# Moving the key and value loads of batches 1 to 7 from the ScalarE queue to the SyncE queue in a fused attention and mixture-of-experts kernel

## The chip, the cores and the metric

The kernel runs on one core of one Trainium2 chip. The metric is the device time of one execution in microseconds (us), as the median over runs. One further execution was taken by the hardware profiler; every time below that is not called a run's time comes from that profile and counts from the start of its span.

## What is computed

Two stages, the second fed by the first:

```
q: (8, 16, 384, 64)   k, v: (8, 1, 384, 64)      # 16 query heads share one key/value head
attn = softmax(q @ k^T / 8) @ v                  # per batch and head
x    = attn laid out as (8*384, 16*64) = (3072, 1024)

g    = argmax(x @ w_group)                       # 4 groups, top 1
e    = argmax(x @ w_expert[g])                   # 4 experts in the group, top 1
out  = p_group * p_expert * (relu(x @ w1[g,e]) @ w2[g,e])     # w1, w2: 1024 x 1024 each
```

All inputs and the output are fp32. For each token only the chosen expert counts.

## The kernel before

The work is tiled by batch (8 batches of 384 tokens) and, within a batch, by three query chunks of 1024 columns. The program walks over 24 chunks; its loop variable is `p` (L409), with `b, r = divmod(p, 3)` the batch and the chunk within it, and `g = 2 * p` and `g + 1` the two halves of the chunk. The order of instructions on each engine is written out by hand (the pools are under a manual schedule), so a queue runs its instructions in the order in which the program text issues them.

One pass through the loop does, in this order:

- `scores` (L188) for half `g`, key tiles 0 and 1: TensorE multiplies keys by queries into the PSUM tile `s` (two buffers), and ScalarE takes the exponential into `pt` (L195). A third `s` tile has to wait until ScalarE has read the first.
- `stats_q` (L161): one ScalarE pass over the raw queries of `p`. After it, `load_q(p + 3)` (L73) issues four DMAs from SyncE into the raw-query buffer that `p` used (three buffers, so the load waits for `stats_q(p)` and for the transpose of `p`).
- Where r is 1: `gate_a` (L271), the router's matmuls for the batch before, with a ScalarE copy.
- On VectorE: `pre_add` (L200, adds the exponentials of the key tiles into `presum`), `prep_q(p + 1)` (L179, transposes the next chunk's queries into `qT`) and, where r is 2, `prep_k(b + 1)` (L175, the next batch's keys into `kT`).
- On TensorE: `values` (L249, `pt` times `v`) for the previous chunk, and the softmax denominators of the previous chunk. Up to chunk 6 these come from `sum_keys` (L223: matmuls into `kss`, transposed by VectorE into `krow`, L230) and `invert` (L233: small matmuls `sm` from `krow`, L238, then a reciprocal and a transpose). From chunk 7 on, VectorE folds the sums instead (`fold_keys`, L213).
- `scores` for key tile 2 of half `g` and tile 0 of half `g + 1`, then `weigh(p - 1)` (L258), which writes the attention output `xT`, a bf16 copy of it by GpSimd and, at the end of a batch, a store of it to DRAM from SyncE (L267).
- From chunk 7 on (`MOE_AT`, L408), `fill` (L398) puts units of the expert stage between the attention pieces: `h_unit` (L348, eight matmuls with `w1` and a ReLU on ScalarE) and `y_unit` (L357, eight matmuls with `w2`, a scaled copy on ScalarE, and a store of `y` from SyncE, L380).
- `scores` for key tiles 1 and 2 of half `g + 1`. Where r is 1, `gate_c` (L319) finds the expert that most tokens of the batch before chose and has GpSimd load that expert's weights (L95, L331).
- At the end of the pass, where r is 0: `load_kv(b + 1)` (L83). It issues four key DMAs (48 KB each, the keys written twice into a layout of 32-row pieces) and one value DMA (96 KB). Keys and values have two buffers each. The keys are transposed two passes later by `prep_k(b + 1)`, and the values are first read four passes later, by `values`.

Batch 0's keys are loaded from ScalarE before the loop and its values from SyncE. All other loads of keys and values go from ScalarE, behind the exponentials of the pass and ahead of those of the next. Queries, the router's weights (`gw`, L152 to L154), the stores of `x_bf` and all stores of `y` go from SyncE; expert weights go from GpSimd.

The framework gives the DMAs of SyncE and ScalarE together eight completion semaphores, by turns, in the order in which it plans them. A DMA that gets a semaphore waits on its own engine until the DMA that had the semaphore before has landed. The listing of the kernel's instructions shows these waits; for batch 3, loaded at the end of pass 6, the four key DMAs and the value DMA wait in ScalarE's stream for the semaphores numbered 6, 0, 1, 2 and 3, and numbers 2 and 3 were last given to the first two of the four query loads of chunk 9, which SyncE issues in the same pass.

Of the kernel before, what the change touches and what calls it, by code (L numbers as in the profile page):

```python
# [21 lines left out]
def kernel(  # L22
# [11 lines left out]
    nc = tc.nc  # L34
# [7 lines left out]
    ST = S // P  # L42
# [16 lines left out]
    kv = k.rearrange("b o (k i) (j d) -> b o j i k d", i=32, j=2)  # L59
# [23 lines left out]
    def load_kv(b):  # L83
        kt = pool.tile([P, NB, 32], FP32, tag="k", name="k")
        for a in range(2):
            for j in range(2):
                nc.scalar.dma_start(out=kt[64 * a + 32 * j:64 * a + 32 * j + 32], in_=kv[b, 0, j])
        k_raw[b] = kt
        vt = pool.tile([P, ST, D], FP32, tag="v", name="v")
        (nc.sync if b == 0 else nc.scalar).dma_start(out=vt[:], in_=v[b, 0].rearrange("(st p) d -> p st d", st=ST))  # L90
        v_sb[b] = vt

    def load_w1(w1, e):
# [10 lines left out]
    make_identity(nc, ident)  # L104
    load_q(0, 2)
    load_kv(0)

    one = singles.tile([P, 1], FP32, name="one")
# [300 lines left out]
    for p in range(NP + 1):  # L409
        b, r = divmod(p, RP)  # L410
# [80 lines left out]
        if r == 0 and b + 1 < B:  # L491
            load_kv(b + 1)
# [262 lines left out]
```

## Time and profile before

The runs take 509.71 us in the median (508.79 to 510.08, three runs). The profiled execution has a span of 507.9 us.

| engine | busy, us | share of the span |
|---|---|---|
| TensorE matmul (PE) | 482.7 | 95% |
| TensorE weight load (PEld, overlaps PE) | 205.1 | 40% |
| VectorE (DVE) | 345.0 | 68% |
| ScalarE (ACT) | 241.6 | 48% |
| GpSimd (POOL) | 63.7 | 13% |

In the lines of the profile, a group or a piece of the timeline is named by engine, source line, operation and `out<-in` tiles, `xN` being how many instructions are merged. In the timeline the first number is the start and the second the duration, both in us; in brackets stands how long the engine sat idle before and what ended it. `ACTq` and `SPq` are the issuing of DMAs on those engines, which the busy time does not count. In the table of waits the three numbers are the total in us, how many waits, and the longest. `PEclk` is the granted TensorE clock as a share of full speed.

### The profile page before, as it was taken

The numbers are of one execution on the slowest core, as the hardware profiler recorded it, in microseconds if no ns is written. First come the engines' busy times: TensorE is split into PE (matmuls) and PEld (weight loads), VectorE is DVE, ScalarE is ACT, GpSimd is POOL, SyncE is SP. The second block draws the span as 40 slices with busy tenths as digits, with TensorE's granted clock in tenths as the row PEclk, the third lists the DMA queues.
The fourth block names the chain that finished last, engine by engine and source line by source line (L and its number), as shares of the span: only waits on it lengthen the run. The fifth ranks groups of instructions, "written<-read, shape, count | busy, mean of one in ns | idle before, by whom it ended". The sixth has DMA issues, their size and how long they took to land. (4 is left out here: it accounts for less than half of the span.)

```text
span 507.9 us, 6898 instructions
## 1 busy us (share of the span) xinstructions
PE 482.7 (95%) x2603; PEld 205.1 (40%) x2623; DVE 345.0 (68%) x480; ACT 241.6 (48%) x341; POOL 63.7 (13%) x64
## 2 busy tenths in 40 slices
PE   8899999969999999999999999999999999998893
PEld 5233333324433443344433444344443444455451
DVE  4588789649974897859975997779974984332100
ACT  4555555245445555545644555454744642322241
POOL 1011113101110020101110120101110210210000
PEclk9999999979999999999999999999999999999997
DMA  9492619963995389845993399647951296599990
GB/s 127 50 126 43 128 29 175 208 129 43 210 183 187 44 139 216 204 87 89 214 205 118 63 182 199 188 83 125 218 129 63 61 205 128 166 245 246 228 243 25
DMA packets 148440, 73.04 MB, mean 144 GB/s; under 512 B 122651, under 2 KB 122651, under 8 KB 148400
## 3 DMA queue, kind: packets, MB, share of 16 engines
q0 software_dynamic: 19008, 37.84, 41.3%
q1 hardware_dynamic: 113792, 32.43, 31.0%
q10 hardware_dynamic: 15600, 2.26, 2.6%
q8 instruction: 22, 0.36, 0.3%
q14 instruction: 18, 0.15, 0.1%
HBM read 91.31 MB, written 19.40 MB: 218 GB/s over the span
## 5 line engine op out<-in xcount | busy, mean ns | idle before, releaser
L195 ACT ACTIVATE pt<-s 128x1024 f32<-128x1024 f32 x144 | 139.8, 1022 | 136.0 <-PE s L193 113.7
L193 PE MATMUL s<-qT,kT 64*128 64x512 f32 x576 | 145.4, 624 | 4.3 <-ACT pt L195 3.4
L256 PE MATMUL o<-pt,v 128*64 128x512 f32 x576 | 130.4, 598 | 0.0
L203 DVE TENSOR_TENSOR presum<-pt 128x1024 f32<-128x1024 f32 x48 | 63.6, 1325 | 46.9 <-ACT pt L195 46.9
L353 PE MATMUL hps<-xbf,w 128*128 128x384 bf16 x512 | 89.3, 326 | 3.8 <-DVE rarei L633 2.0
L362 PE MATMUL yps<-w,hT 128*128 128x512 bf16 x365 | 86.8, 379 | 2.6 <-ACT y L364 1.3
L265 POOL CAST xbf<-xT 128x1024 bf16<-128x1024 f32 x24 | 40.7, 1696 | 326.9 <-DVE xT L264 326.9
L193 PEld LDWEIGHTS s<-qT,kT 64*128 64x128 f32 x576 | 49.3, 187 | 65.0 <-issue 40.6
L256 PEld LDWEIGHTS o<-pt,v 128*64 128x64 f32 x576 | 38.6, 136 | 87.2 <-issue 80.3
L353 PEld LDWEIGHTS <-w 128*128 128x128 bf16 x512 | 48.8, 99 | 46.0 <-issue 16.2
L207 DVE TENSOR_TENSOR presum<-presum,pt 128x1024 f32<-128x1024 f32 x48 | 58.5, 1220 | 2.5
L364 ACT ACTIVATE y<-yps,gsel 128x512 f32<-128x512 f32 x48 | 32.9, 686 | 54.8 <-PE yps L362 48.4
L362 PEld LDWEIGHTS <-hT 128*128 128x128 bf16 x384 | 37.1, 100 | 52.3 <-issue 14.5
L355 ACT ACTIVATE hT<-hps 128x384 bf16<-128x384 f32 x64 | 31.4, 491 | 43.5 <-PE hps L353 41.1
L215 DVE STREAM_TRANSPOSE turn<-presum 128x1024 f32<-128x1024 f32 x34 | 42.3, 1245 | 1.2
L219 DVE TENSOR_REDUCE fold<-turn 128x32 f32<-128x1024 f32 x34 | 41.5, 1220 | 1.2
L184 DVE STREAM_TRANSPOSE qT<-qraw 128x1024 f32<-128x1024 f32 (+1 forms) x25 | 29.9, 1194 | 0.9 <-DMA qraw<-in_q_dram 0.9
L244 DVE STREAM_TRANSPOSE rinv<-rc 128x1024 f32<-128x1024 f32 x24 | 29.9, 1245 | 0.8
L264 DVE TENSOR_TENSOR xT<-o,rinv 128x1024 f32<-128x1024 f32 x24 | 29.4, 1224 | 1.3
L242 DVE RECIPROCAL rc<-sm 128x32 f32<-128x32 f32 x24 | 8.5, 352 | 31.8 <-PE sm L240 21.0
L163 ACT ACTIVATE junk<-qraw 128x1024 bf16<-128x1024 f32 x24 | 25.4, 1059 | 0.0
L95 POOL DMA_DIRECT2D w<-in_moe_w_dram x18 | 12.5, 704 | 66.1 <-DVE gsel L341 45.9
(134 smaller groups left out, 174.9 us busy)
## 6 DMA issues: line engine op xcount, KB each, us to landing
w<-in_moe_w_dram POOLq DMA_DIRECT2D x18, 1024.0 KB, 13.4
w<-in_moe_w_dram POOLq DMA_DIRECT2D x9, 2048.0 KB, 23.7
out_dram<-y SPq DMA_DIRECT2D x48, 256.0 KB, 3.4
qraw<-in_q_dram SPq DMA_DIRECT2D x92, 128.0 KB, 3.8
x_bf<-xbf SPq DMA_DIRECT2D x8, 768.0 KB, 3.3
k<-in_k_dram ACTq DMA_DIRECT2D x32, 48.0 KB, 2.5
xe<-x_bf SPq DMA_DIRECT2D x1, 768.0 KB, 8.9
v<-in_v_dram ACTq DMA_DIRECT2D x7, 96.0 KB, 2.5
```

What stands on the lines that cost most here:

```text
L193: nc.tensor.matmul(out=ps[:, par, :], lhsT=kT[b][r, kt * P:(kt + 1) * P], rhs=qT[g][r, :], start=True, stop=True)
L195: nc.scalar.activation(out=t[:], in_=ps[:], func=ACTF.Exp, scale=scale)
L203: nc.vector.tensor_add(out=t[:], in0=pt[g, 0][:], in1=pt[g, 1][:])
L207: nc.vector.tensor_add(out=t[:], in0=t[:], in1=pt[g, 2][:])
L215: nc.vector.transpose(out=t[:], in_=presum[g][:].rearrange("p a n -> p (a n)"))
L219: nc.vector.reduce_sum(out=fold[p][:, ch, :], in_=t[:].rearrange("p (b i) -> p b i", i=32), axis=AX)
L256: nc.tensor.matmul(out=o_ps[p][64 * par:64 * par + 64, ch, :], lhsT=v_sb[b][:, kt, :], rhs=pt[g, kt][:, par, :], start=(kt == 0), stop=(kt ...
L265: nc.gpsimd.tensor_copy(out=xbf[b][:, cs], in_=xT[b][:, cs])
L353: nc.tensor.matmul(out=ps[:, 0:S], lhsT=w1[:, ko, fc * P:(fc + 1) * P], rhs=xb[:, ko * S:(ko + 1) * S], start=(ko == 0), stop=(ko == KO - 1))
L355: nc.scalar.activation(out=state["h"][:, fc, :], in_=ps[:, 0:S], func=ACTF.Relu)
L362: nc.tensor.matmul(out=ps[:], lhsT=state["h"][:, fo, st * P:(st + 1) * P], rhs=w2[:, fo, nh * CW:(nh + 1) * CW], start=(fo == 0), stop=(fo ...
L364: nc.scalar.activation(out=y, in_=ps[:], func=ACTF.Copy, scale=gs[:, st:st + 1])
```

## The change

`load_kv` issues the keys and values of batches 1 to 7 from SyncE; those of batch 0 stay where they were. Its purpose is to keep DMA issue, and whatever a DMA waits for before it is issued, out of ScalarE's instruction stream, where the exponentials queue behind it.

```diff
         for a in range(2):
             for j in range(2):
-                nc.scalar.dma_start(out=kt[64 * a + 32 * j:64 * a + 32 * j + 32], in_=kv[b, 0, j])
+                (nc.scalar if b == 0 else nc.sync).dma_start(out=kt[64 * a + 32 * j:64 * a + 32 * j + 32], in_=kv[b, 0, j])
         k_raw[b] = kt
         vt = pool.tile([P, ST, D], FP32, tag="v", name="v")
-        (nc.sync if b == 0 else nc.scalar).dma_start(out=vt[:], in_=v[b, 0].rearrange("(st p) d -> p st d", st=ST))
+        nc.sync.dma_start(out=vt[:], in_=v[b, 0].rearrange("(st p) d -> p st d", st=ST))
```

In the instruction streams this takes 35 DMAs (28 for keys, 7 for values) out of ScalarE's and puts them into SyncE's: for batch 1 ahead of the loads of query chunk 4, and for each later batch b after the stores that come before it in pass 3(b - 1) and ahead of the load of query chunk 3(b - 1) + 4. VectorE, TensorE and GpSimd keep their order. Since the semaphores are dealt out by turns, the numbers that a DMA gets and waits for change too: in the changed kernel, after the first DMAs, no instruction of ScalarE's stream waits for a DMA of SyncE just to issue one of its own.

## Prediction

> **What bounds the kernel now.** I read the page first, then the waits, and then the timeline at each of the seven loads that move. On the page:
>
> ```profile
> PE 482.7 (95%) x2603; PEld 205.1 (40%) x2623; DVE 345.0 (68%) x480; ACT 241.6 (48%) x341; POOL 63.7 (13%) x64
> ...
> PEclk9999999979999999999999999999999999999997
> ...
> k<-in_k_dram ACTq DMA_DIRECT2D x32, 48.0 KB, 2.5
> ```
>
> TensorE is busy 95% of the span, so a ScalarE that is 48% busy bounds nothing on average. All that freeing ScalarE can return is time in which TensorE stood still, or ran slowly, because of it. The clock row has one dip before the end, in its ninth slice (102 to 114 us). The waits:
>
> ```profile
> ACT pt L195 <- DMA k<-in_k_dram: 18.3, 6, 8.3
> ...
> PE sm L238 <- DVE krow L230: 4.4, 1, 4.4
> PE s L193 <- ACT pt L195: 3.4, 9, 1.3
> ```
>
> Exponentials stood behind key loads six times, 18.3 us in all, one of them 8.3 us. TensorE has only two waits of note: 4.4 us for `krow` and a longest of 1.3 us for `pt`. The timeline shows whether they belong together. Around the load of batch 3:
>
> ```profile
> 94.28 0.32 ACTq L87 DMA_DIRECT2D k<-in_k_dram  x1
> ...
> 94.64 7.25 ACTq L87 DMA_DIRECT2D k<-in_k_dram  x3
> ...
> 103.25 0.39 ACTq L90 DMA_DIRECT2D v<-in_v_dram  x1
> 103.68 1.94 ACT L195 ACTIVATE pt<-s 128x1024 f32<-128x1024 f32 x2 [8.32 <-DMA k<-in_k_dram]
> ...
> 105.65 1.23 DVE L203 TENSOR_TENSOR presum<-pt 128x1024 f32<-128x1024 f32 x1 [5.96 <-ACT pt L195]
> ...
> 107.96 0.68 DVE L230 STREAM_TRANSPOSE krow<-kss 128x512 f32<-128x512 f32 x1
> 108.78 0.62 PE L238 MATMUL sm<-krow,selq 128*64 128x16 f32 x8 [4.36 <-DVE krow L230]
> ```
>
> Read downwards, this is one chain: key DMAs hold ScalarE from 94.6 to 103.6, VectorE waits 5.96 us for the exponentials, `krow` stands in VectorE's order behind them, and TensorE waits 4.36 us for `krow`. The clock and DMA share in stretches of 4 us (the third and fourth numbers from the end):
>
> ```profile
> 100.00:104.00 4.00, 4.00 (x24) 0.93 (x20) 0.00 (x0) 0.32 (x1) 0.00 (x0) 1.00 1.20 214
> 104.00:108.00 4.00, 0.41 (x2) 0.00 (x0) 2.35 (x3) 3.02 (x5) 0.00 (x0) 0.84 0.47 143
> 108.00:112.00 4.00, 3.22 (x14) 1.73 (x16) 3.06 (x5) 0.55 (x1) 0.00 (x0) 0.50 0.85 121
> 112.00:116.00 4.00, 4.00 (x25) 2.25 (x22) 1.70 (x8) 2.13 (x4) 1.04 (x1) 0.80 0.02 4
> ```
>
> The gap also cost clock: half speed from about 106.7 to 113.6 (0.84, 0.50 and 0.80 are averages over stretches partly at 0.5). Until 104 the DMA engines are full, with the first expert's weights, which GpSimd issues from 76.0 on. Around the load of batch 1:
>
> ```profile
> 18.43 0.48 ACTq L90 DMA_DIRECT2D v<-in_v_dram  x1
> 18.96 1.94 ACT L195 ACTIVATE pt<-s 128x1024 f32<-128x1024 f32 x2 [1.38 <-PE s L193]
> 20.04 2.04 PE L193 MATMUL s<-qT,kT 64*128 64x512 f32 x8 [1.28 <-ACT pt L195]
> ```
>
> Here the exponentials start when the value DMA has been issued, though `s` was ready, and TensorE waits 1.28 us.
>
> [...]at 94.6 three key DMAs of at most 1.1 us each fill 7.25 us, with gaps. [...]a gap of 4.36 us is followed by half clock, and gaps of 1.3 us and less are not.
>
> **The change, part by part.** It takes 35 DMA issues out of ScalarE's stream. At a median of 0.48 us each they are 17 us of ScalarE, plus the waits in between at batch 3. What each of the seven places is worth is what TensorE lost there.
>
> *Batch 1 (16.5 us).* Without the loads, `exp` starts as in other passes 1.18 us after its matmul (14.46 to 15.64): 16.72 + 1.18 = 17.90 instead of 18.96. The matmul that waits for it follows 1.08 us later (20.04 - 18.96), at 18.98 instead of 20.04: 1.06 us gained. The 0.2 us left is the 0.27 us that stands in nearly every early pass.
>
> *Batch 2 (53.5 us).* The exponentials start 1.39 us late, but TensorE goes from scores to the router's matmuls (55.73), `values` (57.16) and scores (59.89) without idling: nothing gained, hidden by those 4.2 us of matmuls.
>
> *Batch 3 (94.3 us).* The scores matmuls of 94.50 are done at about 95.6 and 96.6, so the two exponentials end at about 97.7. VectorE is busy to 99.7, then `presum` 1.2, `qT` 1.2 (its queries were issued by 75.5) and `krow` 0.7: done at about 102.8. TensorE ends `values` at 104.4 and finds `krow` ready. The 4.36 us vanish, and with them the half clock. Its price from the rows: the eight scores matmuls take 109.33 to 113.05, 3.72 us, against 1.92 us in an undisturbed pass (168.16 to 170.08): 1.80; the `sm` group 0.55 against 0.29 (25.64 to 25.93): 0.26; the first matmuls after it 0.54 against 0.32: 0.22. Sum 2.3. From the clock itself: half speed from 108.8 to 113.6 is 2.4. I take 2.3, so 6.7 us here.
>
> *Batches 4 to 7 (161, 216, 273, 328 us).* ScalarE is held about 2 us each time, but TensorE runs 5.37 us of `values` meanwhile:
>
> ```profile
> 272.81 1.97 ACTq L87 DMA_DIRECT2D k<-in_k_dram  x4
> 274.54 5.37 PE L256 MATMUL o<-pt,v 128*64 128x512 f32 x24
> 275.40 1.94 ACT L195 ACTIVATE pt<-s 128x1024 f32<-128x1024 f32 x2 [1.93 <-DMA k<-in_k_dram]
> ```
>
> The next matmul starts at 279.74 without idling: nothing gained four times.
>
> *What it adds.* About 2.5 us of issue in SyncE's stream per batch. Queued behind are the query load of chunk p + 4 and later the stores of `y`. That query load waits for `stats_q` on ScalarE anyway: in pass 15 the last store goes out at 273.50 and the query load at 278.40, and its issue takes 0.3 us, so over 4 us lie open for 2.5 us of issue. The value load's new wait for TensorE's `values` of the batch two before is over by then. The worst place is batch 3: SyncE itself is stuck in the query loads of chunk 9 until 101.15 and in a store until 102.4. The keys then go out by about 104.5 and land by about 108; `prep_k` reads them at 129.04, about 121 in the new time. The next queries go out at about 107 as before and are read at 143.62. At batch 1 SyncE even starts earlier: its loads of `gw` waited from 14.73 to 18.36 for a key DMA's semaphore. Keys then go out at about 25 to 27 and are read at 35.59. So the added work costs 0. Bound from above: the longest issue of one query load took 13.6 us; should SyncE be held that much longer, queries (two passes, 25 us or more) would still be in time and the keys of batch 3 (13 us from landing to reading) only just.
>
> Sum: 1.06 + 4.36 + 2.3 = 7.7 us; 509.7 - 7.7 = 502.0. After batch 3 the rest is paced by TensorE, with no idle stretch above 0.2 us until 436 us, and weight loads are released by the same stream, so all of it moves forward together.
>
> **Rivals.** *(a) Only half of batch 3's loss returns*: another wait of 2 to 3 us takes the place of `krow`, or the clock still drops. Against it: 1.6 us of slack between `krow` and its reader. 509.7 - 1.1 - 4.4 = 504.3. *(b) The stall stays*, because the full DMA engines, not ScalarE, hold TensorE through late queries. Against it: the queries `qT` needs at 106.79 were issued by 75.5. Only batch 1 returns: 508.6. *(c) Slower*: in-order SyncE now blocks where ScalarE did, keys or queries arrive late during a weight load, and TensorE gets new gaps that drop the clock. Two gaps like that of batch 3 are 2 x 6.7 = 13.4 against 7.7 returned: 515.4. For it: SyncE sat in query issues for over 10 us several times. Against it: slack of 13 us and more each time.
>
> **How the numbers follow.** Main case 0.78 (500.6 to 503.2, the terms of the sum each being uncertain by some tenths and the runs by 1.3 us), (a) 0.12, (b) 0.05, (c) 0.05. Predicted 502.0. The range goes from 500.6 to 505.5, which takes in (a). Faster by over 0.3% is below 508.2: main case and (a), 0.90; (b) is within 0.3%: 0.05; slower 0.05.
>
> **What would show it.** Right: no wait of `pt` for key DMAs after batch 0; the 4.4 us wait of `sm` gone; the clock row without its dip in the ninth slice; the scores matmul near 19 us instead of 20.04; no new wait of VectorE for `qraw` or `k`. The forecast is wrong if TensorE shows a new gap of over 2 us, or if VectorE's transposes wait for DMA.

## The result, and the profile after

| | median, us | runs, us | ratio to before |
|---|---|---|---|
| before | 509.89 | 508.79 to 510.09 (4) | |
| loads on SyncE | 502.85 | 501.29 to 503.45 (4) | 0.9861 (95%: 0.9835 to 0.9888) |

The changed kernel is 7.0 us faster. The profiled execution spans 501.3 us (507.9 before). From its page, the busy times, the clock row and the two rows of DMA issues:

```profile
PE 484.2 (97%) x2623; PEld 205.5 (41%) x2623; DVE 345.2 (69%) x480; ACT 241.3 (48%) x341; POOL 63.7 (13%) x64
...
PEclk9999999999999999999999999999999999999898
...
k<-in_k_dram SPq DMA_DIRECT2D x28, 48.0 KB, 2.6
...
v<-in_v_dram SPq DMA_DIRECT2D x8, 96.0 KB, 2.5
```

Nobody does less work (20 matmul records are missing from the trace before, so its 482.7 us of TensorE may be a little low). The dip of the ninth slice is gone, and a small new one stands in the 38th. A key DMA takes 2.6 us from issue to landing, against 2.5 us when ScalarE issued it. From the waits:

```profile
DVE presum L203 <- ACT pt L195: 33.2, 21, 4.6
...
ACT L167 <- DMA k<-in_k_dram: 6.4, 1, 6.4
...
PE s L193 <- ACT pt L195: 2.3, 9, 0.3
...
PE hps L353 <- DVE rarei L633: 2.0, 1, 2.0
...
DVE kT L177 <- DMA qraw<-in_q_dram: 2.0, 1, 2.0
```

The waits of `pt` for key DMAs and of `sm` for `krow` no longer occur. The one wait of ScalarE for keys is batch 0's at the start, which the change leaves. VectorE's wait for `presum` fell by 13.7 us (46.9 before), TensorE's longest wait for `pt` from 1.28 to 0.3 us. VectorE's wait for the first loads, 2.0 us, was there before (1.8 us), and it has no later wait of note for queries or keys. The timeline at the load of batch 3:

```profile
85.02 15.05 SPq L80 DMA_DIRECT2D qraw<-in_q_dram  x4
...
94.72 1.94 ACT L195 ACTIVATE pt<-s 128x1024 f32<-128x1024 f32 x2 [0.31 <-PE s L193]
...
100.67 2.80 PE L256 MATMUL o<-pt,v 128*64 128x512 f32 x12
100.72 2.65 SPq L87 DMA_DIRECT2D k<-in_k_dram  x4
100.96 0.67 DVE L230 STREAM_TRANSPOSE krow<-kss 128x512 f32<-128x512 f32 x1
...
103.30 0.36 PE L238 MATMUL sm<-krow,selq 128*64 128x16 f32 x8
```

The same chain as before, now in time: the exponentials start 0.31 us after `s`, `krow` is done at 101.63, and TensorE is still in `values` until 103.47, so `sm` follows without a gap. SyncE is stuck in the query loads of chunk 9 until 100.07, and the keys go out behind them from 100.72 to 103.37, where nobody needs them until 121.75. The clock in the stretches that were at 0.84, 0.50 and 0.80 before (third number from the end):

```profile
104.00:108.00 4.00, 4.00 (x27) 2.29 (x24) 3.79 (x8) 1.94 (x2) 1.04 (x1) 1.00 1.08 161
108.00:112.00 4.00, 4.00 (x23) 1.80 (x21) 3.63 (x8) 3.06 (x5) 0.00 (x0) 1.00 0.18 19
112.00:116.00 4.00, 4.00 (x25) 2.06 (x22) 3.69 (x12) 1.66 (x4) 1.49 (x3) 1.00 0.04 4
```

TensorE is busy throughout and at full clock. Following TensorE's own instructions through both traces shows where the time is won (starts in us; the lead is before minus after):

| TensorE's instruction | before | after | lead |
|---|---|---|---|
| second scores pair of batch 0 | 9.76 | 9.90 | -0.14 |
| scores held at batch 1 | 20.04 | 19.11 | 0.93 |
| scores ahead of batch 3's load | 94.50 | 93.55 | 0.95 |
| `sm` that waited for `krow` | 108.78 | 103.30 | 5.48 |
| scores after the next `hps` | 116.41 | 108.63 | 7.78 |
| `yps` that waits for `L` | 436.31 | 428.53 | 7.78 |
| `hps` that waits for `rarei` | 473.13 | 465.35 | 7.78 |

The `yps` row of the table in TensorE's timeline, before first:

```profile
436.31 1.89 PE L362 MATMUL yps<-w,hT 128*128 128x512 bf16 x8 [0.31 <-DVE L L297]
```

```profile
428.53 1.89 PE L362 MATMUL yps<-w,hT 128*128 128x512 bf16 x8 [0.31 <-DVE L L297]
```

A lead of 7.78 us is won by 109 us and kept for 350 us. Part of it is lost in the next group, here in both traces, TensorE's timeline, before first:

```profile
473.13 9.26 PE L353 MATMUL hps<-xbf,w 128*128 128x384 bf16 x56 [2.02 <-DVE rarei L633]
```

```profile
465.35 10.94 PE L353 MATMUL hps<-xbf,w 128*128 128x384 bf16 x56 [2.03 <-DVE rarei L633]
```

The same 56 matmuls after the same wait take 1.68 us longer. The lead of 6.10 us that is left stays to the last store, which starts at 500.79 us before and at 494.69 after. The stretches of the changed kernel there say why:

```profile
466.00:467.00 1.00, 1.00 (x6) 0.54 (x5) 0.00 (x0) 0.02 (x1) 0.00 (x0) 0.78 1.09 266
467.00:468.00 1.00, 1.00 (x4) 0.45 (x3) 0.00 (x0) 0.47 (x1) 0.00 (x0) 0.50 1.14 213
...
469.00:470.00 1.00, 1.00 (x5) 0.49 (x4) 0.00 (x0) 0.46 (x1) 0.00 (x0) 0.52 1.13 215
470.00:471.00 1.00, 1.00 (x8) 0.61 (x7) 0.00 (x0) 0.03 (x1) 0.00 (x0) 1.00 1.12 211
```

The clock is at half from 466.55 to 469.97, 3.42 us: the new dip in the clock row. It follows a wait that the kernel before had too (2.02 us), without such a dip in its profile.

### The profile page after: what moved, and what is told of

It reads as the page before. It is cut to its first block, busy times and chain, and to the rows that moved or that the text cites. A ratio compares the mean times of both kernels' runs of the same rounds, so it can differ in the third digit from the quotient of the medians.

```text
span 501.3 us, 6937 instructions
## 1 busy us (share of the span) xinstructions
PE 484.2 (97%) x2623; PEld 205.5 (41%) x2623; DVE 345.2 (69%) x480; ACT 241.3 (48%) x341; POOL 63.7 (13%) x64
## 5 line engine op out<-in xcount | busy, mean ns | idle before, releaser
L193 PE MATMUL s<-qT,kT 64*128 64x512 f32 x576 | 143.6, 617 | 2.7 <-ACT pt L195 2.3
L353 PE MATMUL hps<-xbf,w 128*128 128x384 bf16 x512 | 90.8, 330 | 3.8 <-DVE rarei L633 2.0
L362 PE MATMUL yps<-w,hT 128*128 128x512 bf16 x384 | 89.5, 379 | 1.6 <-ACT y L364 1.3
```

The costliest lines, as they stand in the source:

```text
L193: nc.tensor.matmul(out=ps[:, par, :], lhsT=kT[b][r, kt * P:(kt + 1) * P], rhs=qT[g][r, :], start=True, stop=True)
L353: nc.tensor.matmul(out=ps[:, 0:S], lhsT=w1[:, ko, fc * P:(fc + 1) * P], rhs=xb[:, ko * S:(ko + 1) * S], start=(ko == 0), stop=(ko == KO - 1))
L362: nc.tensor.matmul(out=ps[:], lhsT=state["h"][:, fo, st * P:(st + 1) * P], rhs=w2[:, fo, nh * CW:(nh + 1) * CW], start=(fo == 0), stop=(fo ...
```

## The experiments

The theory: batch 3's gap and its half clock are one loss of some 6.7 us, caused by ScalarE's stream standing in DMA waits while an exponential queued behind; batch 1 adds 1.06 us; the other five loads add nothing; SyncE has room. The rivals: the cost is the issue time of 35 DMAs, not a wait; or something else about batch 3 holds TensorE; or the SyncE side takes back part of the gain. The runs of the kernel before beside the first four experiments have a median of 508.83 us (9 runs), beside the other four of 509.51 us (15 runs). To compare inside the profiles, I use as a landmark the start of the `yps` matmul that waits for `L` (436.31 us before, 428.53 us after), which lies ahead of the dip near the end.

**Only batch 3 on SyncE.** Against the changed kernel:

```diff
-                (nc.scalar if b == 0 else nc.sync).dma_start(out=kt[...], in_=kv[b, 0, j])
+                (nc.sync if b == 3 else nc.scalar).dma_start(out=kt[...], in_=kv[b, 0, j])
...
-        nc.sync.dma_start(out=vt[:], ...)
+        (nc.sync if b in (0, 3) else nc.scalar).dma_start(out=vt[:], ...)
```

> Only the load of batch 3 moves to SyncE; the other six stay on ScalarE. My theory: batch 3 is worth 4.36 us of gap and 2.3 us of clock, so about 503.1 us, the wait of sm for krow gone, the wait of 1.28 us at the scores matmul near 20.0 still there, and the matmul yps that waits for L near the end (436.31 before, 428.53 changed) at about 429.5. Rival, the issue time of all 35 DMAs is what returns: one seventh of the gain, about 508.9.

Measured: 503.92 us (502.07 to 504.31), ratio 0.9892 (0.9871 to 0.9914), the `yps` landmark at 429.87. From TensorE's timeline:

```profile
20.42 2.04 PE L193 MATMUL s<-qT,kT 64*128 64x512 f32 x8 [1.26 <-ACT pt L195]
...
104.63 0.36 PE L238 MATMUL sm<-krow,selq 128*64 128x16 f32 x8
```

The wait at batch 1 is back, 1.26 us, and `sm` has no gap. One load of seven brings 6.44 of the 7.78 us (436.31 - 429.87); of the 1.34 us left, 0.26 us is this execution's later start (second scores pair at 10.16 instead of 9.90) and 1.08 us is batch 1. The loads of batches 2 and 4 to 7 bring nothing that shows: the table of waits still has exponentials behind key DMAs five times, 9.3 us in all, and TensorE doesn't wait with them:

```profile
ACT pt L195 <- DMA k<-in_k_dram: 9.3, 5, 2.1
```

**All on SyncE but batch 3.** The reverse:

```diff
-                (nc.scalar if b == 0 else nc.sync).dma_start(out=kt[...], in_=kv[b, 0, j])
+                (nc.scalar if b in (0, 3) else nc.sync).dma_start(out=kt[...], in_=kv[b, 0, j])
...
-        nc.sync.dma_start(out=vt[:], ...)
+        (nc.scalar if b == 3 else nc.sync).dma_start(out=vt[:], ...)
```

> All loads but that of batch 3 move. By the instruction listing, the four keys of batch 3 now get semaphores whose last users have long landed, and only its value DMA waits for the first query load of chunk 9, which landed at 101.55 before and should land about 1 us earlier here. My theory: ScalarE is held until about 101.0 instead of 103.7, sm waits about 2.7 us instead of 4.36[...]: 1.0 from batch 1, 1.7 from the shorter gap, 2.3 from the clock, about 504.8 us; with the clock dropping all the same about 507. Rival, issue time: six sevenths of the gain, about 503.8 with the gap unchanged in length. Rival, the full DMA engines hold TensorE: gap as before, 508.8.

Measured: 505.92 us (504.37 to 507.60), ratio 0.9942 (0.9922 to 0.9962), landmark 431.49. Timeline, ScalarE and its queue, then TensorE, and the stretch with the gap:

```profile
93.61 1.66 ACTq L87 DMA_DIRECT2D k<-in_k_dram  x3
...
100.66 0.40 ACTq L90 DMA_DIRECT2D v<-in_v_dram  x1
101.10 1.94 ACT L195 ACTIVATE pt<-s 128x1024 f32<-128x1024 f32 x2 [6.78 <-DMA k<-in_k_dram]
...
106.20 0.41 PE L238 MATMUL sm<-krow,selq 128*64 128x16 f32 x8 [2.82 <-DVE krow L230]
```

```profile
104.00:108.00 4.00, 1.80 (x16) 1.03 (x16) 3.37 (x5) 0.73 (x3) 0.00 (x0) 1.00 1.11 225
```

Batch 3's stall returns, though smaller. The semaphores are dealt out anew, so the four keys now go out in 2.0 us and the value DMA alone waits for a query DMA of SyncE, from 95.3 to 100.66. The exponentials are held 6.78 us in place of 8.32, and the gap is 2.82 us in place of 4.36: both shrank by the same 1.54 us. In this execution (504.37 us) the clock stays at 1.00 from 100 to 116, so half clock is a separate price that did not come with this gap of 2.82 us. The six runs reach from 504.37 to 507.60, with mean clocks from 0.994 down to 0.989, the longest run having the lowest. Some of them may have dropped the clock at the gap, but only the one of 504.37 has a trace, and the mean clock alone doesn't tell (see the sum, below).

**Only the two waiting DMAs of batch 3 on SyncE.** Does the issue time count, or the wait? Three keys of batch 3 and everything of the other batches go back to ScalarE, 33 DMAs; the fourth key and the value DMA stay on SyncE. Before, these two waited 5.92 us (95.65 to 101.57) and 1.36 us (101.89 to 103.25), each until one of the first two query loads of chunk 9 had landed (101.55 and 103.22):

```diff
-                (nc.scalar if b == 0 else nc.sync).dma_start(out=kt[...], in_=kv[b, 0, j])
+                (nc.sync if b == 3 and a == 1 and j == 1 else nc.scalar).dma_start(out=kt[...], in_=kv[b, 0, j])
...
-        nc.sync.dma_start(out=vt[:], ...)
+        (nc.sync if b in (0, 3) else nc.scalar).dma_start(out=vt[:], ...)
```

> As before, except that the fourth key DMA and the value DMA of batch 3, the two that wait for query loads of chunk 9, are issued from SyncE; 33 of the 35 DMAs stay on ScalarE. My theory: the wait was the cost, not the issue, so the same as moving the whole load of batch 3: about 503.1 us, no wait of sm for krow, the exponentials starting by 96. Rival, issue time: two of 35, no change that can be measured, 509.5.

Measured: 503.85 us (502.15 to 504.31), ratio 0.9893 (0.9872 to 0.9913), landmark 429.73. Timeline of ScalarE and TensorE:

```profile
94.89 1.00 ACTq L87 DMA_DIRECT2D k<-in_k_dram  x2
95.94 1.94 ACT L195 ACTIVATE pt<-s 128x1024 f32<-128x1024 f32 x2 [0.34 <-PE s L193]
...
104.49 0.36 PE L238 MATMUL sm<-krow,selq 128*64 128x16 f32 x8
```

Two DMAs of 35 bring what all five of batch 3 bring (503.92, landmark 429.87). ScalarE still spends 1.36 us on three keys, and the exponentials start 0.34 us after `s` regardless. The issue-time rival falls: the landmark moved by 6.58 us because ScalarE no longer waited for SyncE's query DMAs.

**Nineteen DMAs per load instead of five.** Has SyncE room? In the changed kernel, each load of batches 1 to 7 is cut into 16 key and 3 value DMAs, same bytes:

```diff
-                (nc.scalar if b == 0 else nc.sync).dma_start(out=kt[...], in_=kv[b, 0, j])
+                for i in range(1 if b == 0 else 4):
+                    c = slice(0, NB) if b == 0 else slice(3 * i, 3 * i + 3)
+                    (nc.scalar if b == 0 else nc.sync).dma_start(out=kt[..., c], in_=kv[b, 0, j, :, c])
...
-        nc.sync.dma_start(out=vt[:], ...)
+        for st in range(1 if b == 0 else ST):
+            c = slice(0, ST) if b == 0 else slice(st, st + 1)
+            nc.sync.dma_start(out=vt[:, c], ...)
```

> The changed kernel with each load of batches 1 to 7 cut into 16 key DMAs and 3 value DMAs on SyncE: 19 issues instead of 5, some 7 to 9 us of SyncE per batch instead of 2.5. My theory, SyncE has room: same time as the changed kernel within 0.5 us, about 502.9, with no wait of VectorE for keys or queries after the start. Rival, SyncE was already near its limit: queries or keys late, gaps of TensorE of some us per batch, 507 or more.

Measured: 501.36 us (501.30 to 503.55), ratio 0.9866 (0.9843 to 0.9889), landmark 428.58. SyncE's timeline at batch 2, and the waits of its queue for `stats_q`, in the changed kernel and in this one (whose source lines stand up to four further down):

```profile
56.08 9.61 SPq L89 DMA_DIRECT2D k<-in_k_dram  x16
```

```profile
SPq L80 <- ACT junk L163: 85.8, 12, 13.6
```

```profile
SPq L80 <- ACT junk L167: 54.3, 9, 9.6
```

A load now takes some 11 us of SyncE instead of 2.5 (9.61 and 1.33 for the values), and the landmark is within 0.05 us of the changed kernel's. What shrank is SyncE's waiting for `stats_q`, from 85.8 to 54.3 us. The rival in which SyncE takes back part of the gain falls, even at four times the work that the change adds. In this profile the 56 matmuls behind the wait for `rarei` take 9.26 us, not 10.94, which the last section comes back to.

**ScalarE held on purpose.** If the wait is the whole cause, useless work on ScalarE at that place must make the loss again with all loads on SyncE. In the changed kernel, at the end of pass 6, with n = 4, 6 and 9 (extra work only, nobody reads it):

```diff
+        if p == 6:
+            for _ in range(n):
+                spin = pool.tile([P, 2 * CW], BF16, tag="junk", bufs=1, name="spin")
+                nc.scalar.activation(out=spin[:]..., in_=ident[:]... .to_broadcast([P, 8, P]), func=ACTF.Square)
```

> The changed kernel with four ScalarE activations of no use (a square of the identity into the scratch tile of the statistics, 0.92 us apart) at the end of pass 6, where the load of batch 3 stood: ScalarE is held 3.7 us, but waits for no DMA. In the changed profile the exponentials there end 1.9 us before VectorE takes them, and krow is ready 1.7 us before TensorE does. My theory: a hold up to about 3.6 us is free, so at most 0.3 us over the changed kernel, about 503.1. Rival, every us of ScalarE at that place counts: plus 3.7, about 506.6.

> Six such activations, a hold of 5.5 us. My theory: sm waits 5.5 - 3.6 = 1.9 us for krow and the clock stays: plus 1.9, about 504.8. With a drop of the clock all the same: plus 4, about 507.

> Nine such activations, a hold of 8.3 us, about what the DMA waits held before. My theory: sm waits about 4.7 us, the clock drops, plus 4.7 and 2.3 to 2.6: about 510, so the loss of batch 3 is made again with no DMA on ScalarE. Rival, the loss needs the DMA wait itself or the full DMA engines: about 503 to 505.

| n | held, us | gap of `sm`, us | half clock after it | landmark | median (range), us | ratio to before |
|---|---|---|---|---|---|---|
| 4 | 4.32 | no wait shown | no | 429.01 | 502.66 (501.41 to 503.29) | 0.9866 (0.9842 to 0.9890) |
| 6 | 6.50 | 2.31 | no | 431.11 | 504.96 (503.78 to 505.85) | 0.9918 (0.9897 to 0.9940) |
| 9 | 9.76 | 5.57 | about 105.8 to 112.6 | 436.09 | 509.59 (508.62 to 510.35) | 1.0004 (0.9995 to 1.0014) |

The timelines of n = 6 and n = 9, ScalarE and TensorE, and the clock row of n = 9:

```profile
94.34 6.50 ACT L496 ACTIVATE spin<-ident 128x1024 bf16<-128x1024 f32 x6
...
105.82 0.41 PE L238 MATMUL sm<-krow,selq 128*64 128x16 f32 x8 [2.31 <-DVE krow L230]
```

```profile
94.39 9.76 ACT L496 ACTIVATE spin<-ident 128x1024 bf16<-128x1024 f32 x9
...
109.14 0.62 PE L238 MATMUL sm<-krow,selq 128*64 128x16 f32 x8 [5.57 <-DVE krow L230]
```

```profile
PEclk9999999979999999999999999999999999999997
```

With no load on ScalarE, 9.76 us of other work put the gap, the dip in the ninth slice and the old time back. From n = 6 to n = 9 the hold and the gap grow by the same 3.26 us. The first 4 us or so are nearly free: n = 4 sets the landmark back by 0.48 us. One activation took 1.08 us, where I had planned with 0.92, so the holds are longer than meant and the gaps a little above those expected. For n = 6 and 4 the clock is at 1.00 in every stretch from 100 to 116 us, and the runs of n = 6 form two pairs about 1.7 us apart; the pair with the higher times (505.62 and 505.85) also has the lower mean clock, 0.991 against 0.995; neither of that pair has a trace.

**The wait near the end moved.** In the changed kernel, the read of `rarei` into registers, for which `hps` waited 2.03 us, is put behind the last units of the main path:

```diff
-    rare = nc.values_load(rarei[0:1, 0:1], min_val=0, max_val=2, ...)
...
     while begun[0] < B or units:
         fill(1)
+    rare = nc.values_load(rarei[0:1, 0:1], min_val=0, max_val=2, ...)
```

> The changed kernel with the read of the rare-case flag (the wait of hps for rarei, 2.03 us, after which the changed profile runs 3.4 us at half clock) moved behind the last expert units, where VectorE has long computed it. My theory: the 2.0 us return, and with them the 1.7 us that the half clock cost in the changed profile, if the dip follows from that gap: 3.7 us in the runs that have the dip, about 499.2, and 2.0 in those that do not. Rival: the wait only moves to the end, 502.9.

Measured: 500.39 us (500.31 to 500.76), ratio 0.9825 (0.9809 to 0.9842); the landmark, ahead of the edit, is at 428.62. TensorE's timeline, and the clock row:

```profile
463.78 9.26 PE L353 MATMUL hps<-xbf,w 128*128 128x384 bf16 x56 [0.36 <-ACT hT L355]
...
487.28 3.61 PE L652 MATMUL py<-w,hc 128*128 128x512 bf16 x16 [0.30 <-DMA w<-in_moe_w_dram]
```

```profile
PEclk9999999999999999999999999999999999999998
```

The 56 matmuls take 9.26 us again, the dip is gone, and the runs lie within 0.45 us where the changed kernel's spread over 2.16. It is faster than both kernels, by 2.46 us in the median than the changed one (2.1 us if the two series are set level by the kernel before, 509.89 and 509.51 us). The forecast of 499.2 us was too low by 1.2 us: 0.36 us of the old wait are left and the last weights now arrive 0.30 us late, and another 0.27 us is the last store, which ends 6.91 us after its start instead of 6.64; the rest was not traced.

## Why the prediction was right, by its own steps

**Batch 1.** Forecast 1.06 us; the wait went from 1.28 to 0.21 us, 1.07. As this execution began 0.14 us late, the matmul stands at 19.11, "near 19".

**Batches 2 and 4 to 7.** Forecast nothing. The lead is 0.93 us at batch 1 and 0.95 us ahead of batch 3's load, with batch 2 between them, and stays at 7.78 us from 109 to 465 us. The first experiment agrees: with these loads on ScalarE as before, only batch 1's part is missing.

**Batch 3's gap.** Forecast 4.36 us, on the ground that `krow` would be ready 1.6 us ahead of its reader. It was done at 101.63 and read at 103.30, 1.7 us. The lead rose by 4.53 us at this place (5.48 - 0.95), 4.36 from the gap; the other 0.17 us is that `sm` now starts at 103.30, ahead of the modelled end of `values` at 103.47. That it was the wait and not the issue time of the DMAs is shown by the two-DMA version, and that the wait alone suffices by the 9.76 us of useless work.

**Batch 3's clock.** Forecast 2.3 us. The lead rose by another 2.30 us (7.78 - 5.48) while the stretches went back to 1.00. That the sizes match so well has some luck in it: the price was read from one execution, and the last section shows a wait of 2.02 to 2.03 us with half clock behind it in the changed kernel and without it in the kernel before. Other executions of the kernel before may have paid less; none of them was traced. The forecast's reading also passed over the start of that dip: 106.74 us, 2.32 us after TensorE fell idle at 104.42 and 2.04 us before its next matmul.

**What SyncE takes on.** Forecast nothing, with keys of batch 3 out by 104.5 and read at 121: they were out by 103.37 and read at 121.75. At batch 1 the keys went out from 23.81 to 26.02 and the values by 26.54, a little ahead of the "25 to 27" of the forecast, and were read at 34.66. A key DMA took 2.6 us from issue to landing, against 2.5 us from ScalarE. The change saved more than ScalarE's issue time: it also moved two waits, of 5.92 and 1.36 us, off the engine that TensorE depends on, and these two DMAs alone moved the landmark by 6.58 us.

**The rivals.** (a), half of batch 3 only, is excluded by the clock row, which keeps full speed there, and by `sm` without a gap, though the version with batch 3 alone on ScalarE shows that such a middle case exists (2.82 us of gap, no half clock). (b) is excluded by the disappearance of the wait although the DMA engines were still about full there (a share of 0.95 from 100 to 104 us and of 1.08 from 104 to 108), (c) by the absence of new waits, and also by the nineteen DMAs.

**The sum and the 0.85 us.** The forecast sum was 7.7 us and the lead 7.78 us. The median is 502.85 instead of 502.0, and one term that was not in the sum accounts for it in the profiled execution. The step that missed it is "so all of it moves forward together": it looked for idle stretches up to 436 us and not at the 2.02 us wait for `rarei` behind them. The list of TensorE's "two waits of note" leaves this wait out too, though the table of waits before has it, as 2.0 us, longer than the 1.3 us that was priced. That wait moved along, but in the profiled execution half clock followed it, which cost 1.68 us (10.94 us for the 56 matmuls, 9.26 before). The four runs would fit: 502.82 (the profiled one), 503.45 and 502.87 us at mean clocks of 0.992 to 0.993, and 501.29 us at 0.995. But the mean clock can't decide it. A half-clock stretch of 3.42 us lowers the mean by 0.5 x 3.42 / 501 = 0.003, and so does the half clock behind the last matmul, which takes the last 5.17 us of the span before (from 502.69) and the last 4.06 us in the changed kernel (from 497.27); the four runs of the last experiment lie within 0.45 us at mean clocks from 0.994 to 0.997. That the run of 501.29 is one without the dip is therefore a guess from its time and not seen in a trace. That the dip comes from the wait is supported by the last experiment: with the wait shortened to 0.36 us the dip is gone, and its four runs spread over 0.45 us.

## What to carry to other kernels

The completion semaphores that two DMA queues share by turns coupled their engines here: one key DMA held ScalarE's compute for 5.92 us, until a query load of SyncE had landed. So look for DMA issues that last longer than an issue and ask whose landing they wait for. Price such a hold only where it outlasts the work that the bounding engine still has (here 4.32 us of hold set the landmark back by 0.48 us, and from 6.50 to 9.76 us of hold the gap grew by the same 3.26 us, plus the clock where it dropped), which made one load of seven worth nearly all of the change. When a schedule shifts, look again at the gaps that were harmless: the wait of 2.02 us near the end had no half clock behind it before, and 3.42 us of it in the changed kernel.

## What the runs showed of the hardware

The length of TensorE's idle gap did not tell by itself whether half clock came with it. The wait for `rarei` is 2.02 to 2.03 us long in all these kernels but the last one, and the same 56 matmuls of `hps` stand behind it:

| kernel | wait for `rarei`, us | the 56 matmuls behind it, us |
|---|---|---|
| changed kernel | 2.03 | 10.94 |
| only batch 3 on SyncE | 2.02 | 10.94 |
| two DMAs on SyncE | 2.03 | 10.94 |
| all but batch 3 | 2.02 | 9.26 |
| nineteen DMAs | 2.03 | 9.26 |
| four activations | 2.02 | 9.26 |
| six activations | 2.03 | 9.26 |
| nine activations | 2.02 | 9.26 |
| before | 2.02 | 9.26 |

In the changed kernel the 1.68 us more are the half clock from 466.55 to 469.97; in the kernel before, the clock is at 1.00 from 113.57 to 502.69 us. The gaps of `sm` behind `krow`:

| kernel | gap, us | granted clock |
|---|---|---|
| six activations | 2.31 | 1.00 from 100 to 116 us |
| all but batch 3 | 2.82 | 1.00 from 100 to 116 us |
| before | 4.36 | 0.50 from 106.74 to 113.57 us |
| nine activations | 5.57 | 0.50 from about 105.8 to 112.6 us |

The last row is worked out from the means of its stretches: 0.73 from 104 to 108 us, 0.50 from 108 to 112 and 0.92 from 112 to 116. So a gap of 2.82 us passed at full clock, while half clock followed one of 2.03 us. What else decides was not shown. Each kernel was traced once, so it also stays open whether the wait for `rarei` goes one way in some executions of a kernel and the other way in others, which could explain why runs of one kernel lie about 2 us apart.
